# Fixing the engine order and putting all loads of an attention-plus-FFN kernel on one queue

The change has three parts. The program's own order of instructions is kept on every engine instead of a scheduler's. All loads go through one DMA queue in the order in which they are thought to be needed. The FFN weights arrive as f32 in column halves and are cast on GpSimd, where they had been cast to f16 by the DMA itself.

## Chip, cores and metric

One core of one Trainium2 chip. The metric is device time in microseconds (us), median of the runs. The kernel before takes 393.2 us (3 runs, 393.12 to 394.5).

## The reference

```python
def _attn_ref(q, k, v):                       # q, k, v: (8, 12, 448, 64) f32
    scores = (1 / sqrt(64)) * q @ k^T
    m = max(scores);  e = exp(scores - m)
    attn = e / (sum(e) + exp(-m) + 1e-9)      # = exp(s) / (sum exp(s) + 1)
    return attn @ v
# x = attention output as (3584, 768): token rows, 12 heads side by side
def _moe_ref(x, w1, w2, w3, w_out):           # each w 768 x 768 f32
    h = max(x @ w1, x @ w2, x @ w3)
    return h @ w_out
```

## The kernel before

A group is four heads of one batch; there are 24 groups, three per batch. Per group: load q, k, v (three tiles of 448 KB), cast to f16 on GpSimd, transpose q and k on TensorE, scores into PSUM, Exp on ScalarE (eight of 0.82 us), then denominator and numerator. Once three groups of a batch are done, the FFN pieces of that batch fill TensorE between the attention of the next. A first-layer piece is six matmuls, about 1.14 us.

```python
    def load_weight(i):                      # GpSimd's queue; the DMA casts f32 -> f16
        w = (moe_w1, moe_w2, moe_w3, moe_w_out)[i]
        if i < 3:
            src = w.rearrange("(hh gf dd) f -> hh dd gf f", hh=GH, dd=32)
            for hh in range(GH):             # four DMAs, 32 partitions each
                nc.gpsimd.dma_start(out=w_sb[i][hh*32 : hh*32+32], in_=src[hh])
        else:
            nc.gpsimd.dma_start(out=w_sb[i], in_=w.rearrange("(dc p) f -> p dc f", p=128))
# ... [cut: cast_group, transpose_group, scores_visit, av_group, up_piece, out_piece]
    cast_group(0)
    for i in range(4):
        load_weight(i)
    transpose_group(0)
    cast_group(1)
    for i in range(NI):                      # NI = 24 groups
        if i + 2 < NI: load_group(i + 2)     # SyncE's queue
        for vi, (pr, cs) in enumerate(visits):
            scores_visit(i, pr, cs)
            moe(per_visit)                   # FFN pieces that are due
            if vi == 0 and i > 0:
                av_group(i - 1)              # then add_pieces(b - 1) after each third group
            if vi == 2 and i + 1 < NI: transpose_group(i + 1)
        if i + 2 < NI: cast_group(i + 2)
```

The softmax here doesn't subtract the row's maximum and nothing guards it: scores larger than these inputs give would overflow.

Of the kernel before, what the change touches and what calls it, by code (L numbers as in the profile page):

```python
# [10 lines left out]
FP32 = mybir.dt.float32  # L11
FP16 = mybir.dt.float16
AF = mybir.ActivationFunctionType
ALU = mybir.AluOpType
ts = bass.ts

MMDT = FP16
LAMBDA = 256.0
# [3 lines left out]
def kernel(  # L22
# [11 lines left out]
    nc = tc.nc  # L34

    B, H, S, D = q.shape
    NTOK, DM = out.shape
    DFF = moe_w1.shape[1]
    SC = 112
    NCH = S // SC  # L40
    NDC = DM // 128
    NFC = DFF // 128
    GH = 4
    NG = H // GH
# [6 lines left out]
            name=nc.get_next_instruction_name(),  # L51
# [5 lines left out]

    cpool = ctx.enter_context(tc.tile_pool(name="const", bufs=1))
    ld_pool = ctx.enter_context(tc.tile_pool(name="ld", bufs=3))
    p16_pool = ctx.enter_context(tc.tile_pool(name="p16", bufs=2))  # L60
    v16_pool = ctx.enter_context(tc.tile_pool(name="v16", bufs=3))
    att_pool = ctx.enter_context(tc.tile_pool(name="att", bufs=4))
    e_pool = ctx.enter_context(tc.tile_pool(name="e", bufs=2))
    small = ctx.enter_context(tc.tile_pool(name="small", bufs=2))
    xt_pool = ctx.enter_context(tc.tile_pool(name="xt", bufs=2))
# [3 lines left out]
    ps1 = ctx.enter_context(tc.tile_pool(name="ps1", bufs=4, space=bass.MemoryType.PSUM))  # L69
    ps2 = ctx.enter_context(tc.tile_pool(name="ps2", bufs=2, space=bass.MemoryType.PSUM))  # L70

    groups = [(b, g) for b in range(B) for g in range(NG)]
    raw = {}

    def load_group(i):
        b, g = groups[i]
        tiles = []
        for name, src in (("q", q), ("k", k), ("v", v)):
            t = ld_pool.tile([SC, GH, NCH, D], FP32, tag="ld_" + name, name="ld_" + name)
            nc.sync.dma_start(  # L80
                out=t.rearrange("p h c d -> p h (c d)"),
                in_=src[b].rearrange(
                    "(h g) (p c) d -> g p h (c d)", g=NG, c=NCH
                )[g],
            )
            tiles.append(t)
        raw[i] = tiles

    load_group(0)
    load_group(1)  # L90

    ident16 = cpool.tile([128, 128], MMDT, name="ident16")
    make_identity(nc, ident16)
# [5 lines left out]
    w_sb = [cpool.tile([128, NDC, DFF], MMDT, name=f"w{i}") for i in range(4)]  # L99
    wout_sb = w_sb[3]  # L100

    def load_weight(i):
        w = (moe_w1, moe_w2, moe_w3, moe_w_out)[i]
        if i < 3:
            src = w.rearrange("(hh gf dd) f -> hh dd gf f", hh=GH, dd=32)
            for hh in range(GH):
                nc.gpsimd.dma_start(
                    out=w_sb[i][hh * 32 : hh * 32 + 32], in_=src[hh]
                )
        else:  # L110
            nc.gpsimd.dma_start(
                out=w_sb[i], in_=w.rearrange("(dc p) f -> p dc f", p=128)
            )


    state = {}

    def cast_group(i):
        qf, kf, vf = raw.pop(i)
        qk16 = []  # L120
        for pr in range(GH // 2):
            q16 = p16_pool.tile([SC, NCH, 2, D], MMDT, tag=f"q16_{pr}", name=f"q16_{pr}")
            k16 = p16_pool.tile([SC, NCH, 2, D], MMDT, tag=f"k16_{pr}", name=f"k16_{pr}")
            nc.gpsimd.tensor_copy(  # L124
                out=q16, in_=qf[:, 2 * pr : 2 * pr + 2].rearrange("p h c d -> p c h d")
            )
            nc.gpsimd.tensor_copy(  # L127
                out=k16, in_=kf[:, 2 * pr : 2 * pr + 2].rearrange("p h c d -> p c h d")
            )
            qk16.append((q16, k16))  # L130
        v16 = v16_pool.tile([SC, GH, NCH, D], MMDT, tag="v16", name="v16")
        nc.gpsimd.tensor_scalar(
            out=v16, in0=vf, scalar1=LAMBDA, scalar2=None, op0=ALU.mult
        )
        state[i] = {"qk16": qk16, "v16": v16}

    def transpose_group(i):
        st = state[i]
        st["qkT"] = []
        for pr in range(GH // 2):  # L140
            q16, k16 = st["qk16"][pr]
            trT = ps1.tile([128, 2, S], MMDT, tag="bank1", name="trT")
            for c in range(NCH):
                nc.tensor.transpose(  # L144
                    out=trT[:, 0, ts(c, SC)], in_=q16[:, c, :, :],
                    identity=ident16[0:SC, 0:SC],
                )
                nc.tensor.transpose(  # L148
                    out=trT[:, 1, ts(c, SC)], in_=k16[:, c, :, :],
                    identity=ident16[0:SC, 0:SC],  # L150
                )
            qkT = att_pool.tile([2 * D, 2, S], MMDT, tag="qkT", name="qkT")
            nc.vector.tensor_copy(out=qkT, in_=trT)  # L153
            st["qkT"].append(qkT)
        del st["qk16"]

    def scores_visit(i, pr, cs):
        st = state[i]
# [25 lines left out]
    def av_group(i):  # L184
        b, g = groups[i]
        st = state.pop(i)
        eT, v16 = st["eT"], st["v16"]
        if g == 0:
            xT[b] = xt_pool.tile([128, NDC, S], MMDT, tag="xT", name="xT")

        def col_tiled(weights):
            bank = ps1.tile([128, 512], FP32, tag="bank1", name="av")
            for c in range(NCH):
                for hh in range(GH):
                    nc.tensor.matmul(  # L195
                        out=bank[32 * hh : 32 * hh + 32, 0:S],
                        lhsT=weights(hh, c),
                        rhs=eT[:, hh, c, :],
                        start=(c == 0),
                        stop=(c == NCH - 1),  # L200
                    )
            return bank

        den = col_tiled(lambda hh, c: ones16[:, :])
        lnd = small.tile([128, S], FP32, tag="lnd", name="lnd")
        nc.scalar.activation(out=lnd, in_=den[:, 0:S], func=AF.Ln, bias=one_b)  # L206
        rb = small.tile([128, S], FP32, tag="rb", name="rb")
        nc.scalar.activation(out=rb, in_=lnd, func=AF.Exp, scale=-1.0)  # L208
        for hf in range(2):
            num = col_tiled(lambda hh, c: v16[:, hh, c, hf * 32 : hf * 32 + 32])  # L210
            nc.vector.tensor_tensor(  # L211
                out=xT[b][:, 2 * g + hf, :], in0=num[:, 0:S], in1=rb, op=ALU.mult
            )
# [23 lines left out]
    NH = 2  # L237
    NW = DM // NH
# [33 lines left out]
    pieces = []  # L272

    def add_pieces(b):
        for fc in range(NFC):
            for i in range(3):
                pieces.append((up_piece, (b, fc, i), NDC * S))
        for t in range(0, 3) if b % 2 == 0 else range(3, 7):
            for nh in range(NH):
                pieces.append((out_piece, (b // 2, t, nh), NFC * NW))  # L280

    credit = [0.0]

    def moe(cols):
        credit[0] += cols
        while pieces and credit[0] > 0:
            f, a, w = pieces.pop(0)
            f(*a)
            credit[0] -= w
        if not pieces:  # L290
            credit[0] = min(credit[0], 0.0)


    per_visit = (3 * NFC * NDC * S + 3.5 * NH * NFC * NW) / (NG * 4)
    cast_group(0)
    for i in range(4):
        load_weight(i)
    transpose_group(0)
    cast_group(1)

    visits = [(pr, cs) for pr in range(2) for cs in ((0, 1), (2, 3))]
    NI = len(groups)
    for i in range(NI):
        b, g = groups[i]
        if i + 2 < NI:
            load_group(i + 2)
        for vi, (pr, cs) in enumerate(visits):
            scores_visit(i, pr, cs)
            moe(per_visit)
            if vi == 0 and i > 0:  # L310
                av_group(i - 1)
                if g == 0:
                    add_pieces(b - 1)
            if vi == 2 and i + 1 < NI:
                transpose_group(i + 1)
        if i + 2 < NI:
            cast_group(i + 2)
    av_group(NI - 1)
    add_pieces(B - 1)
    moe(float("inf"))  # L320

# [29 lines left out]
```

## Time and profile before

| view | reading |
|---|---|
| busy time | TensorE (PE) 93% of a 390.9 us span |
| first FFN matmul | 51.0 us |
| after it | no gap in PE until 386.2 us; 14.75 us per group |
| longest wait of PE | 13.3 us, for the cast of group 1's q |

PE's waits, longest first: who waited, for what, us in total, times, longest.

```profile
...
PE trT L144 <- POOL q_0_162 L124: 13.3, 1, 13.3
PE trT L144 <- POOL q_0_117 L124: 5.9, 1, 5.9
...
```

GpSimd's own timeline says why that cast came so late: start us, length us, instruction, and in brackets the idle time before it and what ended it.

```profile
...
16.78 0.57 POOL L107 DMA_DIRECT2D w_115<-in_moe_w_dram  x1
21.48 0.57 POOL L107 DMA_DIRECT2D w_115<-in_moe_w_dram  x1 [4.13 <-DMA w_113<-in_moe_w_dram]
...
25.52 0.57 POOL L107 DMA_DIRECT2D w_115<-in_moe_w_dram  x1 [1.50 <-DMA w_113<-in_moe_w_dram]
27.61 0.85 POOL L111 DMA_DIRECT2D w_116<-in_moe_w_out_dram  x1 [1.52 <-DMA w_114<-in_moe_w_dram]
28.46 0.62 POOL L124 CAST q_0_162<-ld_q 112x512 f16<-112x512 f32 x1
...
```

GpSimd stands from 17 to 28 us with the issue of weight DMAs, each of which waits for an earlier one to land. The casts of group 1 (`q_0_162`) come behind them in its order. The data had come earlier: q, k and v of group 1 had landed by 15 us (issue at 2.2, 2.8 and 3.4 us, and 9.4, 10.5 and 11.5 us to landing).

The rates of the DMA engines in some stretches (the last column is GB/s, counted as bytes written): everything up to 49.5 us (the last weight landed at 51 us), weights and q, k, v together from 20 to 28 us, and q, k, v alone from 52 to 64 us.

```profile
...
core 0: us, PE busy (x) PEld busy (x) DVE busy (x) ACT busy (x) POOL busy (x), PEclk, DMA share, GB/s
2.00:49.50 47.50, 26.43 (x249) 11.91 (x253) 7.12 (x12) 23.01 (x31) 29.81 (x38) 1.00 1.13 247
20.00:28.00 8.00, 0.00 (x0) 0.00 (x0) 0.00 (x0) 0.00 (x0) 2.09 (x4) 1.00 1.14 241
52.00:64.00 12.00, 12.00 (x100) 5.91 (x102) 6.43 (x11) 6.19 (x9) 9.70 (x10) 1.00 1.13 274
...
```

Alone, q, k, v came at 274 GB/s.

### The profile page before, as it was taken

The page shows a single profiled execution, that of the slowest core. Times are in us where ns is not written, and L with a number is a line of the kernel's source. Part 1 is how long each engine was busy: PE and PEld are TensorE (multiplying, and loading weights), DVE is VectorE, ACT ScalarE, POOL GpSimd, SP SyncE. Part 2 cuts the span into 40 slices and gives each one's busy share as a digit, 9 for nine tenths or more (in the row PEclk, how much of TensorE's full clock was granted, in tenths as well). Part 3 has the DMA queues.
Part 4 walks back from the last instruction along what each step waited for, and adds up shares of the span by engine and source line. Part 5 has one row for each costly group of instructions (what it writes and reads, how often), then busy time and mean ns, then how long its engine had stood idle before and what let it go on. Part 6 is the DMA issues. An engine that isn't in the chain of part 4 may idle for free.

```text
span 390.9 us, 7477 instructions
## 1 busy us (share of the span) xinstructions
PE 363.1 (93%) x3120; PEld 180.1 (46%) x3120; DVE 174.8 (45%) x298; ACT 194.5 (50%) x241; POOL 129.7 (33%) x139
## 2 busy tenths in 40 slices
PE   2409999999999999999999999999999999999995
PEld 1104344554544554454554554454454554545552
DVE  0003244554454554454544544554554544544553
ACT  1606965556565555555565546556555546552000
POOL 3739666234252243243243233334243220000000
PEclk9999999999999999999999999999999999999998
DMA  8999999935614643527513663437100320004005
GB/s 196 272 240 236 239 285 268 250 85 187 143 47 96 198 152 96 134 71 201 143 47 96 162 189 96 117 74 216 49 3 0 82 82 0 2 0 123 2 0 162
DMA packets 41202, 49.24 MB, mean 126 GB/s; under 512 B 2256, under 2 KB 37584, under 8 KB 41168
## 3 DMA queue, kind: packets, MB, share of 16 engines
q1 hardware_dynamic: 37888, 44.05, 42.6%
q0 software_dynamic: 3280, 4.72, 6.6%
q8 instruction: 24, 0.39, 0.4%
q14 instruction: 10, 0.08, 0.1%
HBM read 42.47 MB, written 11.01 MB: 137 GB/s over the span
## 4 chain that ended last, share of the span: by engine, by line
PE 89%; ACT 2%; POOL 0%; DVE 0%; issue 0%
PE p_i L225 43%; PE op_ps L246 15%; PE av L195 15%; PE stp L166 12%; PE trT L148 2%; PE trT L144 2%; ACT eT L175 2%; ACT rb L208 0%; POOL k_0_163 L127 0%; DVE o_sb L253 0%; ACT lnd L206 0%
## 5 line engine op out<-in xcount | busy, mean ns | idle before, releaser
L175 ACT ACTIVATE eT<-stp 112x896 f16<-112x896 f32 x192 | 164.6, 916 | 126.7 <-PE stp L166 126.7
L235 DVE TENSOR_TENSOR hT<-hT,p_i 128x448 f16<-128x448 f16 x96 | 59.7, 621 | 68.4 <-PE p_i L225 68.3
L225 PE MATMUL p_i<-xT,w_114 128*128 128x448 f16 x288 | 62.9, 353 | 0.0
L225 PE MATMUL p_i<-xT,w_113 128*128 128x448 f16 x288 | 62.8, 353 | 0.0
L225 PE MATMUL p_i<-xT,w_115 128*128 128x448 f16 x288 | 62.5, 353 | 0.0
L166 PE MATMUL stp<-qkT 64*112 64x448 f16 x384 | 60.2, 383 | 1.9 <-ACT eT L175 1.9
L246 PE MATMUL op_ps<-w_116,hT 128*128 128x384 f16 x336 | 59.0, 327 | 0.0
L211 DVE TENSOR_TENSOR xT<-av,rb 128x448 f16<-128x448 f32 x48 | 27.7, 620 | 46.3 <-ACT rb L208 46.3
L253 DVE TENSOR_SCALAR o_sb<-op_ps 128x384 f32<-128x384 f32 x56 | 31.3, 558 | 34.2 <-PE op_ps L246 34.0
L233 DVE CAST hT<-p_i 128x448 f16<-128x448 f32 x48 | 30.0, 625 | 32.6 <-PE p_i L225 32.6
L246 PEld LDWEIGHTS <-hT 128*128 128x128 f16 x336 | 30.8, 98 | 27.0 <-issue 8.1
L153 DVE COPY qkT<-trT 128x896 f16<-128x896 f16 x48 | 27.8, 617 | 29.6 <-PE trT L148 29.6
L225 PEld LDWEIGHTS <-w_115 128*128 128x128 f16 x288 | 26.5, 98 | 29.6 <-issue 7.1
L225 PEld LDWEIGHTS <-w_114 128*128 128x128 f16 x288 | 26.5, 98 | 29.6 <-issue 7.1
L225 PEld LDWEIGHTS <-w_113 128*128 128x128 f16 x288 | 26.7, 98 | 28.9 <-issue 6.1
L166 PEld LDWEIGHTS <-qkT 64*112 64x112 f16 x384 | 18.6, 127 | 34.0 <-issue 24.7
L206 ACT ACTIVATE lnd<-av,one_b 128x448 f32<-128x448 f32 x24 | 15.3, 638 | 32.9 <-PE av L195 32.9
L195 PE MATMUL av<-eT,ones_109 112*32 112x448 f16 x384 | 25.8, 360 | 0.0
L195 PEld LDWEIGHTS <-ones_109 112*32 112x32 f16 x384 | 8.6, 96 | 14.1 <-issue 10.5
L208 ACT ACTIVATE rb<-lnd 128x448 f32<-128x448 f32 x24 | 13.9, 578 | 0.8
L144 PE MATMUL trT<-ident_104,q_0_162 112*128 112x112 f16 x4 | 0.9, 294 | 13.3 <-POOL q_0_162 L124 13.3
L144 PEld LDWEIGHTS <-q_0_162 112*128 112x128 f16 x4 | 0.5, 130 | 13.8 <-POOL q_0_162 L124 13.8
(371 smaller groups left out, 289.8 us busy)
## 6 DMA issues: line engine op xcount, KB each, us to landing
ld_q<-in_q_dram SPq DMA_DIRECT2D x24, 448.0 KB, 4.5
ld_k<-in_k_dram SPq DMA_DIRECT2D x24, 448.0 KB, 5.9
ld_v<-in_v_dram SPq DMA_DIRECT2D x24, 448.0 KB, 4.0
out_dram<-o_sb SPq DMA_DIRECT2D x8, 336.0 KB, 3.0
out_dram<-o_sb SPq DMA_DIRECT2D x8, 288.0 KB, 4.1
out_dram<-o_sb SPq DMA_DIRECT2D x8, 240.0 KB, 4.1
out_dram<-o_sb SPq DMA_DIRECT2D x8, 192.0 KB, 2.7
w_113<-in_moe_w_dram POOLq DMA_DIRECT2D x4, 288.0 KB, 9.1
```

Of the source, the lines that this page charges most:

```text
L153: nc.vector.tensor_copy(out=qkT, in_=trT)
L166: nc.tensor.matmul(out=stp[:, hh, 0:S], lhsT=qkT[hh * D : hh * D + D, 1, ts(c, SC)], rhs=qkT[hh * D : hh * D + D, 0, :], start=True, stop= ...
L175: nc.scalar.activation(out=st["eT"][:, 2 * pr : 2 * pr + 2, c, :], in_=stp[:, :, 0:S], func=AF.Exp, scale=scale,)
L195: nc.tensor.matmul(out=bank[32 * hh : 32 * hh + 32, 0:S], lhsT=weights(hh, c), rhs=eT[:, hh, c, :], start=(c == 0), stop=(c == NCH - 1),)
L206: nc.scalar.activation(out=lnd, in_=den[:, 0:S], func=AF.Ln, bias=one_b)
L208: nc.scalar.activation(out=rb, in_=lnd, func=AF.Exp, scale=-1.0)
L211: nc.vector.tensor_tensor(out=xT[b][:, 2 * g + hf, :], in0=num[:, 0:S], in1=rb, op=ALU.mult)
L225: nc.tensor.matmul(out=p_i[:, 0:S], lhsT=w_sb[i][:, dc, ts(fc, 128)], rhs=xT[b][:, dc, :], start=(dc == 0), stop=(dc == NDC - 1),)
L233: nc.vector.tensor_copy(out=dst, in_=p_i[:, 0:S])
L235: nc.vector.tensor_tensor(out=dst, in0=dst, in1=p_i[:, 0:S], op=ALU.max)
L246: nc.tensor.matmul(out=op_ps[:, 0:NW], lhsT=hT[bp][:, fc, ts(t, 128)], rhs=wout_sb[:, fc, ts(nh, NW)], start=(fc == 0), stop=(fc == NFC - 1),)
L253: nc.vector.tensor_scalar(out=o_sb[:, ts(nh, NW)], in0=op_ps[:, 0:NW], scalar1=1.0 / LAMBDA, scalar2=None, op0=ALU.mult,)
```

## The change

Its intent: no GpSimd time for issuing DMAs, no wait of casts behind weights, less waiting of TensorE by an order chosen by hand. The core of the diff, with cuts marked (pools, credits and the finer placing of FFN pieces are left out):

```diff
-    p16_pool ... bufs=2 ; v16_pool ... bufs=3
+    p16_pool ... bufs=4 ; v16_pool ... bufs=5
+    wst_pool = ctx.enter_context(tc.tile_pool(name="wst", bufs=2))
+    ctx.enter_context(tc.manual_schedule())
 ...
+    load_group(0, "qk", 2); load_group(1, "qk"); load_group(0, "v"); load_group(1, "v"); load_group(2)
 ...
-    def load_weight(i):
+    def load_weight(i, half):
+        cols = slice(half * FH, half * FH + FH)
+        wst = wst_pool.tile([128, NDC, FH], FP32, tag="wst", name="wst")
 ...
         if i < 3:
             for hh in range(GH):
-                nc.gpsimd.dma_start(out=w_sb[i][hh * 32 : hh * 32 + 32], in_=src[hh])
+                nc.sync.dma_start(out=wst[hh * 32 : hh * 32 + 32], in_=src[hh][:, :, cols])
+    def cast_weight(i, half):
+        nc.gpsimd.tensor_copy(out=w_sb[i][:, :, cols], in_=wst_of.pop((i, half)))
 ...
+        if i == 0:
+            cast_qk(2); cast_v(2)
+            for w in range(3):
+                load_weight(w, 0); cast_weight(w, 0)
+            load_group(3); cast_qk(3); cast_v(3)
+        elif i == 1:
+            for w in range(3):
+                load_weight(w, 1); cast_weight(w, 1)
+            load_group(4); cast_qk(4); cast_v(4)
+        elif i == 2:
+            for h in range(2):
+                load_weight(3, h); cast_weight(3, h)
+            load_group(5); cast_qk(5); cast_v(5)
 ...
-            if vi == 2 and i + 1 < NI:
-                transpose_group(i + 1)
+            elif vi < 3:                     # visits 1 and 2
+                moe((gap - tr_cols) / 2)
+                if i + 1 < NI:
+                    transpose_pair(i + 1, vi - 1)
+                moe((gap - tr_cols) / 2)
```

In TensorE's fixed order the transposes of group 3 stand in the middle of group 2's scores, and those of group 4 after the first two FFN pieces. On the queue, group 3 stands behind three weight halves and group 4 behind six.

More of the change, by code (lines that the diff above doesn't have):

```diff
@@ L59 @@
     ld_pool = ctx.enter_context(tc.tile_pool(name="ld", bufs=3))
-    p16_pool = ctx.enter_context(tc.tile_pool(name="p16", bufs=2))
-    v16_pool = ctx.enter_context(tc.tile_pool(name="v16", bufs=3))
+    p16_pool = ctx.enter_context(tc.tile_pool(name="p16", bufs=4))
+    v16_pool = ctx.enter_context(tc.tile_pool(name="v16", bufs=5))
     att_pool = ctx.enter_context(tc.tile_pool(name="att", bufs=4))
+    wst_pool = ctx.enter_context(tc.tile_pool(name="wst", bufs=2))
     e_pool = ctx.enter_context(tc.tile_pool(name="e", bufs=2))
@@ L70, with load_group @@
     ps2 = ctx.enter_context(tc.tile_pool(name="ps2", bufs=2, space=bass.MemoryType.PSUM))
+    ctx.enter_context(tc.manual_schedule())
     groups = [(b, g) for b in range(B) for g in range(NG)]
     raw = {}
-    def load_group(i):
+    def load_group(i, which="qkv", step=GH):
         b, g = groups[i]
-        tiles = []
-        for name, src in (("q", q), ("k", k), ("v", v)):
-            t = ld_pool.tile([SC, GH, NCH, D], FP32, tag="ld_" + name, name="ld_" + name)
-            nc.sync.dma_start(
-                out=t.rearrange("p h c d -> p h (c d)"),
-                in_=src[b].rearrange(
-                    "(h g) (p c) d -> g p h (c d)", g=NG, c=NCH
-                )[g],
-            )
-            tiles.append(t)
-        raw[i] = tiles
-    load_group(0)
-    load_group(1)
+        tiles = raw.setdefault(i, {})
+        for name in which:
+            tiles[name] = ld_pool.tile(
+                [SC, GH, NCH, D], FP32, tag="ld_" + name, name="ld_" + name
+            )
+        for h0 in range(0, GH, step):
+            for name in which:
+                src = {"q": q, "k": k, "v": v}[name][b].rearrange(
+                    "(h g) (p c) d -> g p h (c d)", g=NG, c=NCH
+                )[g]
+                nc.sync.dma_start(
+                    out=tiles[name][:, h0 : h0 + step].rearrange("p h c d -> p h (c d)"),
+                    in_=src[:, h0 : h0 + step],
+                )
+    load_group(0, "qk", 2)
+    load_group(1, "qk")
+    load_group(0, "v")
+    load_group(1, "v")
+    load_group(2)
     ident16 = cpool.tile([128, 128], MMDT, name="ident16")
@@ L100 @@
     wout_sb = w_sb[3]
-    def load_weight(i):
+    FH = DFF // 2
+    wst_of = {}
+    def load_weight(i, half):
         w = (moe_w1, moe_w2, moe_w3, moe_w_out)[i]
+        cols = slice(half * FH, half * FH + FH)
+        wst = wst_pool.tile([128, NDC, FH], FP32, tag="wst", name="wst")
+        wst_of[i, half] = wst
         if i < 3:
@@ L106, in load_weight, with cast_qk @@
             for hh in range(GH):
-                nc.gpsimd.dma_start(
-                    out=w_sb[i][hh * 32 : hh * 32 + 32], in_=src[hh]
-                )
-        else:
-            nc.gpsimd.dma_start(
-                out=w_sb[i], in_=w.rearrange("(dc p) f -> p dc f", p=128)
-            )
+                nc.sync.dma_start(
+                    out=wst[hh * 32 : hh * 32 + 32], in_=src[hh][:, :, cols]
+                )
+        else:
+            nc.sync.dma_start(
+                out=wst, in_=w.rearrange("(dc p) f -> p dc f", p=128)[:, :, cols]
+            )
+    def cast_weight(i, half):
+        cols = slice(half * FH, half * FH + FH)
+        nc.gpsimd.tensor_copy(out=w_sb[i][:, :, cols], in_=wst_of.pop((i, half)))
     state = {}
-    def cast_group(i):
-        qf, kf, vf = raw.pop(i)
+    def cast_qk(i):
+        qf, kf = raw[i].pop("q"), raw[i].pop("k")
         qk16 = []
@@ L130, in cast_group, with cast_v, transpose_pair @@
             qk16.append((q16, k16))
+        state[i] = {"qk16": qk16, "qkT": []}
+    def cast_v(i):
         v16 = v16_pool.tile([SC, GH, NCH, D], MMDT, tag="v16", name="v16")
         nc.gpsimd.tensor_scalar(
-            out=v16, in0=vf, scalar1=LAMBDA, scalar2=None, op0=ALU.mult
+            out=v16, in0=raw[i].pop("v"), scalar1=LAMBDA, scalar2=None, op0=ALU.mult
         )
-        state[i] = {"qk16": qk16, "v16": v16}
-    def transpose_group(i):
+        state[i]["v16"] = v16
+    def transpose_pair(i, pr):
         st = state[i]
-        st["qkT"] = []
-        for pr in range(GH // 2):
-            q16, k16 = st["qk16"][pr]
-            trT = ps1.tile([128, 2, S], MMDT, tag="bank1", name="trT")
-            for c in range(NCH):
-                nc.tensor.transpose(
-                    out=trT[:, 0, ts(c, SC)], in_=q16[:, c, :, :],
-                    identity=ident16[0:SC, 0:SC],
-                )
-                nc.tensor.transpose(
-                    out=trT[:, 1, ts(c, SC)], in_=k16[:, c, :, :],
-                    identity=ident16[0:SC, 0:SC],
-                )
-            qkT = att_pool.tile([2 * D, 2, S], MMDT, tag="qkT", name="qkT")
-            nc.vector.tensor_copy(out=qkT, in_=trT)
-            st["qkT"].append(qkT)
-        del st["qk16"]
+        q16, k16 = st["qk16"][pr]
+        trT = ps1.tile([128, 2, S], MMDT, tag="bank1", name="trT")
+        for c in range(NCH):
+            nc.tensor.transpose(
+                out=trT[:, 0, ts(c, SC)], in_=q16[:, c, :, :],
+                identity=ident16[0:SC, 0:SC],
+            )
+        for c in range(NCH):
+            nc.tensor.transpose(
+                out=trT[:, 1, ts(c, SC)], in_=k16[:, c, :, :],
+                identity=ident16[0:SC, 0:SC],
+            )
+        qkT = att_pool.tile([2 * D, 2, S], MMDT, tag="qkT", name="qkT")
+        nc.vector.tensor_copy(out=qkT, in_=trT)
+        st["qkT"].append(qkT)
     def scores_visit(i, pr, cs):
@@ L276, in add_pieces @@
             for i in range(3):
-                pieces.append((up_piece, (b, fc, i), NDC * S))
+                pieces.append((up_piece, (b, fc, i), NDC * (S + 6)))
         for t in range(0, 3) if b % 2 == 0 else range(3, 7):
             for nh in range(NH):
-                pieces.append((out_piece, (b // 2, t, nh), NFC * NW))
+                pieces.append((out_piece, (b // 2, t, nh), NFC * (NW + 6)))
     credit = [0.0]
@@ L291, in moe @@
             credit[0] = min(credit[0], 0.0)
-    per_visit = (3 * NFC * NDC * S + 3.5 * NH * NFC * NW) / (NG * 4)
-    cast_group(0)
-    for i in range(4):
-        load_weight(i)
-    transpose_group(0)
-    cast_group(1)
+    UP = NDC * (S + 6)
+    OUT = NFC * (NW + 6)
+    per_group = (3 * NFC * UP + 3.5 * NH * OUT) / NG
+    av_cols = 3 * NCH * (S + 6) + 480
+    tr_cols = 2 * NCH * SC
+    gap = (per_group + av_cols + 2 * tr_cols) / 4
     visits = [(pr, cs) for pr in range(2) for cs in ((0, 1), (2, 3))]
@@ L302 @@
     NI = len(groups)
+    cast_qk(0)
+    cast_qk(1)
+    cast_v(0)
+    cast_v(1)
+    transpose_pair(0, 0)
+    transpose_pair(0, 1)
     for i in range(NI):
         b, g = groups[i]
-        if i + 2 < NI:
-            load_group(i + 2)
+        if i == 0:
+            cast_qk(2)
+            cast_v(2)
+            for w in range(3):
+                load_weight(w, 0)
+                cast_weight(w, 0)
+            load_group(3)
+            cast_qk(3)
+            cast_v(3)
+        elif i == 1:
+            for w in range(3):
+                load_weight(w, 1)
+                cast_weight(w, 1)
+            load_group(4)
+            cast_qk(4)
+            cast_v(4)
+        elif i == 2:
+            for h in range(2):
+                load_weight(3, h)
+                cast_weight(3, h)
+            load_group(5)
+            cast_qk(5)
+            cast_v(5)
+        elif i + 3 < NI:
+            load_group(i + 3)
+            cast_qk(i + 3)
+            cast_v(i + 3)
@@ L307 @@
         for vi, (pr, cs) in enumerate(visits):
             scores_visit(i, pr, cs)
-            moe(per_visit)
-            if vi == 0 and i > 0:
-                av_group(i - 1)
-                if g == 0:
-                    add_pieces(b - 1)
-            if vi == 2 and i + 1 < NI:
-                transpose_group(i + 1)
-        if i + 2 < NI:
-            cast_group(i + 2)
+            if vi == 0:
+                spare = gap - av_cols
+                moe(spare / 2)
+                if i > 0:
+                    av_group(i - 1)
+                moe(spare / 2)
+                if i > 0 and g == 0:
+                    add_pieces(b - 1)
+            elif vi < 3:
[3 more added lines that the diff above has]
+                moe((gap - tr_cols) / 2)
+            else:
+                moe(gap)
```

## The prediction

> **What bounds the kernel now.** TensorE. The page's busy table gives PE 93% of a 390.9 us span, and the chain of waits is 89% PE. From the first FFN matmul (51.0 us) to the last (386.2 us) PE has no gap: one group of four heads costs 14.75 us, 91.4 to 135.6 us being three of them. After that only a 4.7 us write-out. The change cannot win there: matmuls, tiling switches and tail are the same ones. Only the head, 0 to 51 us, can move.
>
> **Head before.** The wait view: PE waits 5.9 us for the first q cast, then 13.3 us (15.8 to 29.1) for the q cast of group 1. That data had landed (queue 1 moved about 4 MB by 18 us); GpSimd was stuck issuing weight DMAs, each waiting for an earlier one, so its casts came late. Then ScalarE paces two groups (7.8 us each: eight Exp of 0.82, Ln, Exp).
>
> **What the change does.** It removes the weight issues from GpSimd (the 13.3 us hole) and adds eight weight casts there, about 2.5 us each (estimate from 512 columns in 0.61 us), off the critical path. It doubles what the weights write: 4.7 MB of f16 becomes 9.4 MB of f32. And PE's order is now fixed: transposes of group 3 come before scores of group 2 are finished, those of group 4 right after the first two FFN pieces. But on the single queue group 3 stands behind three weight halves and group 4 behind six.
>
> **Arrival sum.** q/k/v alone ran at 275 GB/s (52 to 64 us), 1.67 us a tile. 14 tiles must land before group 4 can be transposed: 23.4 us, plus 3.5 us of start and landing, plus six weight halves of 1.18 MB. Each w1..w3 DMA writes 32 partitions. [...]
>
> **On the critical path.** First transposes about 1.5 us earlier; hole gone; group 1 and 2 run on ScalarE's pace to about 27 us. Then PE waits for group 3's k cast until about 39 us, FFN starts near 48 us (before: 51.0, with exactly the same work done), and after two pieces PE waits again until about 60.5 us for group 4. Before, the equal state was reached at 53.3 us. Net: loss of 7 us[...]. A fixed order also costs about 1 us at batch ends (division waits behind Exps). Group 5 and w_out come in time.
>
> **Prediction:** 400 us, 8 in 10 between 388 and 405. Faster by over 2%: 0.08; within 2%: 0.47; slower by over 2%: 0.45.
>
> **What would show it.** PE's waits: no 13.3 us wait for group 1; instead two for GpSimd casts of groups 3 (about 12 us) and 4 (about 10 us). The 40 slices: queue full from 2 to 65 us[...]. First FFN matmul near 48 us, a hole after its second piece. From about 65 us a group again costs 14.75 us.
>
> **What would make it wrong.** Weight halves arriving faster (above 390 GB/s would make it over 2% faster) or slower; weight casts much over 2.5 us, which would hold back the reuse of the two staging buffers; new PE stalls in the steady part because a fixed order cannot fill waits.

In the arrival sum the rate assumed for the weight halves and its alternative are cut, and so is what rested on them further on: no trace of this case that the prediction had shows them. The sum came to near 60 us for group 4's k: 23.4 us of tiles, 3.5 us of start and landing, and a remainder of about 33 us for the six halves. The 390 GB/s near the end of the text is an estimate from the same sum: six halves at that rate take about 18 us instead of 33.

## More of the kernel before

From the page of the kernel before. In the rows of slices each digit is the busy tenth of 1/40 of the span; PEclk is the granted TensorE clock in tenths; the last row is what the DMA engines wrote, in GB/s.

```profile
span 390.9 us, 7477 instructions
...
PE 363.1 (93%) x3120; PEld 180.1 (46%) x3120; DVE 174.8 (45%) x298; ACT 194.5 (50%) x241; POOL 129.7 (33%) x139
...
PE   2409999999999999999999999999999999999995
...
PEclk9999999999999999999999999999999999999998
...
GB/s 196 272 240 236 239 285 268 250 85 187 143 47 96 198 152 96 134 71 201 143 47 96 162 189 96 117 74 216 49 3 0 82 82 0 2 0 123 2 0 162
...
```

Apart from the write-out at the end, only the head is not full: the first three slices (29 us).

## The result

| | before | after |
|---|---|---|
| median, us | 393.2 | 407.93 (407.56 to 410.06) |
| ratio | | 1.0379, interval 1.0315 to 1.0443: slower |
| first FFN matmul, us | 51.0 | 53.6 |
| first k cast of group 3 / group 4, us | 39.0 / 46.9 | 42.6 / 65.6 |
| written by the DMA engines, mean | 247 GB/s (2 to 49.5 us) | 235 GB/s (2 to 78 us) |

A ratio is the mean time of one kernel's fast runs over the mean of the other's fast runs of the same rounds, so it is not quite the ratio of the medians quoted.

The page of the changed kernel, same lines:

```profile
span 405.8 us, 7489 instructions
...
PE 369.1 (91%) x3120; PEld 180.6 (45%) x3120; DVE 173.9 (43%) x298; ACT 193.1 (48%) x241; POOL 139.1 (34%) x134
...
PE   3980755999999999999999999999999999999995
...
PEclk9996585999999999999999999999999999999999
...
GB/s 195 221 210 216 219 212 303 272 265 47 180 260 88 2 101 265 200 2 40 232 231 26 0 205 274 89 1 88 237 204 2 36 121 2 2 0 118 2 0 156
...
```

The hole of before is gone from slices 2 and 3. In its place stand two, from 31 to 42 us (slices 4 and 5) and from 56 to 64 us (slices 6 and 7), and the granted clock falls in them and is a half just after each (0.50 from 41.5 to 53 us and from 64.4 to 69 us). From slice 8 on both kernels look alike. PE's waits:

```profile
...
PE trT L165 <- POOL q_0_206 L144: 10.9, 1, 10.9
PE trT L165 <- POOL q_0_295 L144: 8.4, 1, 8.4
PE trT L165 <- POOL q_0_130 L144: 4.5, 1, 4.5
...
PE trT L170 <- POOL k_0_296 L147: 1.3, 1, 1.3
PE trT L170 <- POOL k_0_207 L147: 1.2, 1, 1.2
...
```

`q_0_206` is group 3, `q_0_295` is group 4. GpSimd's timeline around them: the casts of weights (`w_126` to `w_128` are w1 to w3) wait for their DMAs, and the two groups come after the weights in arrival and in order.

```profile
...
28.57 2.10 POOL L133 CAST w_126<-wst 128x2304 f16<-128x2304 f32 x1 [3.87 <-DMA wst<-in_moe_w_dram]
33.52 2.11 POOL L133 CAST w_127<-wst 128x2304 f16<-128x2304 f32 x1 [2.85 <-DMA wst<-in_moe_w_dram]
38.85 2.11 POOL L133 CAST w_128<-wst 128x2304 f16<-128x2304 f32 x1 [3.22 <-DMA wst<-in_moe_w_dram]
40.90 0.61 POOL L144 CAST q_0_206<-ld_q 112x512 f16<-112x512 f32 x1
42.62 0.61 POOL L147 CAST k_0_207<-ld_k 112x512 f16<-112x512 f32 x1 [1.10 <-DMA ld_k<-in_k_dram]
...
50.30 2.10 POOL L133 CAST w_126<-wst 128x2304 f16<-128x2304 f32 x1 [2.96 <-DMA wst<-in_moe_w_dram]
55.92 2.11 POOL L133 CAST w_127<-wst 128x2304 f16<-128x2304 f32 x1 [3.52 <-DMA wst<-in_moe_w_dram]
61.71 2.11 POOL L133 CAST w_128<-wst 128x2304 f16<-128x2304 f32 x1 [3.69 <-DMA wst<-in_moe_w_dram]
63.82 0.61 POOL L144 CAST q_0_295<-ld_q 112x512 f16<-112x512 f32 x1
65.63 0.61 POOL L147 CAST k_0_296<-ld_k 112x512 f16<-112x512 f32 x1 [1.20 <-DMA ld_k<-in_k_dram]
...
```

The rates: q, k, v alone (10 to 20 us), weight halves into 32 partitions at a time (22 to 30 and 46 to 60 us), w_out into 128 partitions (67.5 to 71.5 us).

```profile
...
2.00:78.00 76.00, 46.19 (x356) 20.62 (x360) 14.78 (x24) 31.30 (x40) 42.92 (x34) 0.80 1.10 235
10.00:20.00 10.00, 9.07 (x64) 3.80 (x65) 1.25 (x2) 8.35 (x11) 8.28 (x7) 1.00 1.15 220
22.00:30.00 8.00, 6.06 (x80) 2.93 (x78) 1.74 (x3) 7.56 (x10) 4.13 (x2) 1.00 1.11 216
46.00:60.00 14.00, 9.48 (x72) 3.54 (x69) 2.79 (x5) 6.45 (x9) 5.55 (x3) 0.74 1.11 207
67.50:71.50 4.00, 4.00 (x23) 1.61 (x22) 0.81 (x3) 1.73 (x2) 3.76 (x2) 0.68 1.06 372
...
```

The halves come at 216 and 207 GB/s, w_out at 372, and q, k, v alone at 220, not at the 274 that the kernel before showed.

Where the 14.7 us come from (14.9 us between the two profiled spans). Before any experiment the two traces can be lined up. When the changed kernel starts the FFN, exactly the same matmuls have been done as in the kernel before at its FFN start. The first two pieces end at 53.3 us before; after, group 4's k can be transposed at 66.3 us: 13.0 us lost. From there to the end it takes 405.8 - 66.3 = 339.5 us, against 390.9 - 53.3 = 337.6 us before: 1.9 us more, and all of it lies in the first 5 us, in which the clock is still halved (0.50 to 69 us; the run with the longer fill, below, shows this). The steady part costs the same.

### The profile page after: what moved, and what is told of

It is laid out like the page before. It is cut to its first block, busy times and chain, and to the rows that moved or that the text cites. A ratio compares the mean times of both kernels' runs of the same rounds, so it can differ in the third digit from the quotient of the medians.

```text
span 405.8 us, 7489 instructions
## 1 busy us (share of the span) xinstructions
PE 369.1 (91%) x3120; PEld 180.6 (45%) x3120; DVE 173.9 (43%) x298; ACT 193.1 (48%) x241; POOL 139.1 (34%) x134
## 4 chain that ended last, share of the span: by engine, by line
PE 82%; DMA 10%; SPq 4%; POOL 1%; issue 0%; DVE 0%; POOLq 0%
PE p_i L246 42%; PE op_ps L267 14%; PE av L216 12%; PE stp L187 11%; DMA wst<-in_moe_w_dram 8%; SPq L90 3%; DMA ld_k<-in_k_dram 2%; PE trT L170 2%; PE trT L165 2%; SPq L123 2%; POOL w_126 L133 1%; POOL k_0_296 L147 0%; DVE o_sb L274 0%; POOLq L133 0%; POOLq L147 0%
## 5 line engine op out<-in xcount | busy, mean ns | idle before, releaser
L187 PE MATMUL stp<-qkT 64*112 64x448 f16 x384 | 62.0, 393 | 3.9 <-ACT eT L196 3.9
L246 PE MATMUL p_i<-xT,w_126 128*128 128x448 f16 x288 | 63.2, 353 | 0.0
L175 DVE COPY qkT<-trT 128x896 f16<-128x896 f16 x48 | 29.6, 617 | 37.4 <-PE trT L170 37.4
L246 PEld LDWEIGHTS <-w_128 128*128 128x128 f16 x288 | 26.2, 99 | 28.8 <-issue 8.5
L246 PEld LDWEIGHTS <-w_127 128*128 128x128 f16 x288 | 25.9, 98 | 28.3 <-issue 8.0
L246 PEld LDWEIGHTS <-w_126 128*128 128x128 f16 x288 | 26.1, 98 | 27.8 <-issue 6.9
L216 PE MATMUL av<-eT,ones_122 112*32 112x448 f16 x384 | 24.1, 373 | 0.0
L165 PE MATMUL trT<-ident_117,q_0_206 112*128 112x112 f16 x4 | 0.6, 294 | 10.9 <-POOL q_0_206 L144 10.9
L144 POOL CAST q_0_3529<-ld_q 112x512 f16<-112x512 f32 x1 | 0.6, 611 | 27.3 <-DMA ld_q<-in_q_dram 27.3
```

Of the source, the lines that this page charges most:

```text
L175: nc.vector.tensor_copy(out=qkT, in_=trT)
L187: nc.tensor.matmul(out=stp[:, hh, 0:S], lhsT=qkT[hh * D : hh * D + D, 1, ts(c, SC)], rhs=qkT[hh * D : hh * D + D, 0, :], start=True, stop= ...
L216: nc.tensor.matmul(out=bank[32 * hh : 32 * hh + 32, 0:S], lhsT=weights(hh, c), rhs=eT[:, hh, c, :], start=(c == 0), stop=(c == NCH - 1),)
L246: nc.tensor.matmul(out=p_i[:, 0:S], lhsT=w_sb[i][:, dc, ts(fc, 128)], rhs=xT[b][:, dc, :], start=(dc == 0), stop=(dc == NDC - 1),)
```

## The experiments

The theories. **A**: the queue delivers groups 3 and 4 too late, because of how many bytes it must write first and how fast; the fixed order only makes TensorE wait for them. **B**: the fixed order itself costs the time. **C**: the f32 bytes or the GpSimd casts cost it, in whatever order they come. **D**: the halved clock after the waits (0.50 until 53 us and until 69 us) costs it. **E**: the two staging buffers starve the queue. **F** (about the kernel before): its head is bound by bytes, not by GpSimd's issues. All medians are of three rounds unless said.

### Without the fixed order

```diff
-    ctx.enter_context(tc.manual_schedule())
```

> The changed kernel without the line that fixes the order: the scheduler that ordered the kernel before orders each engine again; loads and casts stay as changed. Theory A (late arrival of groups 3 and 4, which stand behind the weights on one queue): casts of group 3 near 41 us and of group 4 near 64 us as in the changed kernel, PE still waits for both, time 404 to 408 us. Rival B (the fixed order of TensorE costs the time): back to 390 to 394 us.

Measured: 405.73 us, ratio 1.0325 (1.0289 to 1.0361). Group 3's k is cast at 42.95 us, group 4's at 64.96. The scheduler moved the rest of group 2's scores ahead of group 3's transposes, and the FFN starts at 49.9 us instead of 53.6, but then waits for group 4 all the same. B falls as the main cause: about 2 of the 14.7 us went with the order, hardly clear of noise (the intervals of the two ratios overlap), and 0.7 us of them is an earlier arrival of group 4.

### Groups 3 and 4 ahead of the weights

```diff
-            for w in range(3): load_weight(w, 0); cast_weight(w, 0)
             load_group(3); cast_qk(3); cast_v(3)
+            for w in range(3): load_weight(w, 0); cast_weight(w, 0)
 ... (the same for group 4 and the second halves)
```

> Same bytes, queue, casts and TensorE order; only groups 3 and 4 are loaded (and cast) ahead of the three weight halves that preceded them. Theory A: no wait for group 3, group 4 cast about 17 us earlier (near 48 us), now the third weight half (near 46 us) and the last halves (near 67 us) are what PE waits for, at about 2 us each; time 389 to 394 us. Rival C (the amount of f32 bytes or the GpSimd casts, whatever their order): still above 400 us.

Measured: 407.48 us, ratio 1.0356 (1.0341 to 1.0372). A miss. The first half came as expected: no wait for group 3, FFN at 40.7 us, group 4's k at 48.6 (after a wait of 4.9 us for its q). The waits for weights that were expected did not come. Instead TensorE stood 13.5 us for group 5, whose k is cast at 80.2 us (78.0 in the changed kernel):

```profile
...
79.22 0.56 PE L165 MATMUL trT<-ident,q 112*128 112x112 f16 x4 [13.53 <-POOL q L144]
...
```

That corrected theory A. The order only chooses which group is late. Through group 5 the queue must write six groups (8.26 MB) and all weights as f32 (9.44 MB), 17.7 MB; at the 235 GB/s of the changed kernel this takes 75 us. The kernel before writes its weights as 4.72 MB. C, as worded ("still above 400"), is right here.

### The same bytes into 128 partitions

Wrong result on purpose: rows of the weights go to the wrong partitions.

```diff
-            src = w.rearrange("(hh gf dd) f -> hh dd gf f", hh=GH, dd=32)
-            for hh in range(GH):
-                nc.sync.dma_start(out=wst[hh * 32 : hh * 32 + 32], in_=src[hh][:, :, cols])
+            src = w.rearrange("(dc p) f -> p dc f", p=128)
+            for d0 in range(0, NDC, 2):
+                nc.sync.dma_start(out=wst[:, d0 : d0 + 2], in_=src[:, d0 : d0 + 2, cols])
```

> Wrong result on purpose: the halves of w1, w2, w3 are read in plain row order, so that each of three DMAs writes all 128 partitions (393 KB each) instead of four DMAs that write 32 partitions each (295 KB each); bytes, row pieces of 1536 B, order and casts are unchanged. Theory A[...]: a half takes 3.2 to 3.6 us instead of 5.65, the weight stretches run at 330 to 370 GB/s as w_out did in the changed kernel, group 4 can be transposed near 52 us, time 392 to 397 us. If 1536 B pieces are slow for another reason: rate stays near 209 GB/s and time near 408 us.

Measured: 401.38 us, ratio 1.0204 (1.0174 to 1.0233). Windows of its trace: two stretches of weights, and the one between them that the expectation had not foreseen.

```profile
...
22.00:26.00 4.00, 2.73 (x28) 1.49 (x25) 1.63 (x3) 3.93 (x5) 2.29 (x2) 1.00 1.05 364
26.00:30.00 4.00, 3.32 (x54) 1.62 (x55) 0.20 (x1) 3.74 (x6) 3.11 (x2) 1.00 0.26 80
42.00:46.00 4.00, 3.43 (x22) 1.55 (x24) 0.62 (x1) 3.94 (x5) 3.44 (x2) 0.50 1.06 373
...
```

The rate is as expected, 364 and 373 GB/s where the changed kernel had 216 and 207, with the same 1536-byte pieces and the same bytes. So in this case the rate goes with the partitions that each DMA writes. The DMAs also grew by a third, from 295 to 393 KB, but the loads of q, k, v, which are larger still (459 KB), ran at 214 to 274 GB/s, so size alone does not make the difference. The time is not as expected: from 26 to 30 us the queue is nearly idle (80 GB/s), because the third half waits for a staging buffer, that is for the cast of the first (25.95 to 28.05 us).

### Unused matmuls in the waits

`fill(n)` (its definition is left out) issues n unused matmuls of 448 columns.

```diff
+                    if vi == 1 and i in (2, 3):
+                        fill({2: 48, 3: 40}[i])      # second run: {2: 54, 3: 70}
                     transpose_pair(i + 1, vi - 1)
```

> 48 unused matmuls before the transposes of group 3 and 40 before those of group 4 keep TensorE busy in its two waits. Theory D (the granted clock of 0.5 after the waits costs time of its own): granted clock 1.0 throughout, FFN starts about 3 us earlier (near 50 us) but then only waits longer for group 4, and the stretch after group 4's transposes shrinks by about 2 us: 405.3 to 406.5 us. Were the half clock the main cause: below 398 us.

Measured: 406.91 us, ratio 1.0368 (1.0324 to 1.0412), 0.4 us above the expected range. The clock still fell (0.50 from 46 to 50 us and from 66 to 68 us), so this run decides little. With a longer fill:

> The changed kernel with more unused matmuls (54 and 70) before the transposes of groups 3 and 4; with 48 and 40 the granted clock had still fallen to 0.5 from 45 to 52 and 65 to 69 us. Theory D: clock 1.0 after 60 us, the six matmuls after group 4's transposes take 1.2 us instead of 2.4, time 404.5 to 406.5 us, so the half clock is worth 1.5 to 3 us of the 14.7 lost.

Measured: 404.83 us, ratio 1.0316 (1.0266 to 1.0366). The same six matmuls after group 4's transposes, in the timeline of PE (start, length, instruction; x6 is a count), first in the changed kernel:

```profile
...
66.30 0.56 PE L170 MATMUL trT<-ident_117,k_0_296 112*128 112x112 f16 x4 [1.25 <-POOL k_0_296 L147]
66.64 2.45 PE L246 MATMUL p_i<-xT,w_128 128*128 128x448 f16 x6
...
```

And in the run with the longer fill:

```profile
...
64.92 0.36 PE L170 MATMUL trT<-ident,k 112*128 112x112 f16 x4
65.12 1.30 PE L246 MATMUL p_i<-xT,w 128*128 128x448 f16 x6
...
```

They take 2.45 us in the changed kernel, at a granted clock of 0.50, and 1.30 us with the longer fill, where the clock row of the page shows 0.9 or more in that slice. Between group 4's k transposes and its second pair of transposes lie 4.99 us in the changed kernel (66.30 to 71.29) and 3.09 us here (64.92 to 68.01), and from there 402.7 - 64.92 = 337.8 us remain, as before the change. So the half clock costs 1.9 us. The rest of the 3 us that this run gained is an earlier arrival of group 4 (63.2 us), not the clock. D is a small part.

### Three staging buffers

```diff
-    wst_pool = ctx.enter_context(tc.tile_pool(name="wst", bufs=2))
+    wst_pool = ctx.enter_context(tc.tile_pool(name="wst", bufs=3))
```

> The changed kernel with three staging buffers for the f32 weights instead of two. In its trace the queue fell to 145 GB/s for 2 us (30 to 32 us) because the third half waited for the cast of the first. Theory A (the queue's rate into 32 partitions): that gives back at most 1 us, 406 to 408 us. Rival E (the reuse of the staging buffers is what starves the queue): below 402 us.

Measured: 409.94 us, ratio 1.0425 (1.0406 to 1.0443); no gain, 2 us above the expected range. The dip at 30 to 32 us is gone (215 GB/s from 28 to 34 us), but q, k, v ran at only 214 GB/s in this profile and group 4's k came at 66.8 us. E is refuted as the main cause. Why the time is not a little better stays open. With 128 partitions it is another matter:

> Wrong result on purpose, as with the 128-partition loads before, now with three staging buffers. With halves of 3.2 us the queue had stood at about 80 GB/s from 26 to 30 us and below 185 from 46 to 50 us, waiting for casts. Theory A with staging as the second limit: those gaps close, group 4's transposes come 3 to 6 us earlier (near 54 us instead of 58 to 59), time 394 to 398 us. If staging does not matter: 401 us as before.

Measured: 395.98 us (wrong result again), ratio 1.0075 (1.0046 to 1.0104), group 4's k at 53.2 us. As expected: with halves of 3.2 us (1.18 MB at 364 to 373 GB/s), two buffers were too few: 401.38 us with two, 395.98 with three.

### The kernel before with one DMA for each weight

Heads of a group are made neighbours and d is split into even and odd, so that partition p of a weight chunk is row 2p plus a constant, and one DMA can fill 128 partitions. The result is correct.

```diff
-  "(h g) (p c) d -> g p h (c d)"
+  "(g h) (p c) d -> g p h (c d)"
-            for hh in range(GH):
-                nc.gpsimd.dma_start(out=w_sb[i][hh * 32 : hh * 32 + 32], in_=src[hh])
+            nc.gpsimd.dma_start(out=w_sb[i].rearrange("p (g hf) f -> p g hf f", hf=2),
+                                in_=w.rearrange("(g p hf) f -> p g hf f", g=NG, hf=2))
 ... (v is cast into a tile with even and odd d apart, and the numerator reads it so)
```

> The kernel before, correct result, with only the layout of heads and of the split of d changed, so that each weight is one casting DMA into 128 partitions (4 DMAs on GpSimd instead of 13). Theory A: GpSimd no longer waits for DMAs in flight, so the 13.3 us wait of TensorE for group 1 is gone; written bytes stay 4.7 MB for the weights; the FFN starts at 38 to 43 us instead of 51; time 381 to 387 us. Rival F (the head is bound by bytes alone, not by GpSimd's queue of issues): FFN starts near 50 us, time 391 to 394 us.

Measured: 397.38 us, ratio 1.01 (1.0061 to 1.0139). A miss. The wait for group 1 is down from 13.3 to 4.4 us, and two others take its place, 6.2 and 4.6 us, both for group 3. The FFN starts at 57.8 us in the profiled run (399.55 us, the slowest of the four); with the granted clock at 0.50 from 44 to 52 us, it takes 13.9 us from group 3's k cast to the FFN, 12.0 in the kernel before. PE's waits in this run:

```profile
...
PE trT L143 <- POOL q L123: 15.8, 3, 6.2
PE trT L147 <- POOL k L126: 6.6, 5, 4.6
...
```

The four weight DMAs now share the DMA engines with q, k, v without a break (227 to 242 GB/s in every 2 us from 16 to 44 us). Group 3's k is cast at 44.0 us, group 2's at 24.95: three tiles (1.38 MB) in 19.0 us are 72 GB/s, while the engines wrote about 233 GB/s in all. How the engines divide their time between the two queues no run here shows. It seems, though no run isolates it, that GpSimd's blocked issues, which looked like the whole trouble of the kernel before, had also kept the weights from crowding out q, k, v (group 3's k was cast at 39.0 us there). F is nearer the truth than A was.

### The changed kernel with casting DMAs

Fixed order and the order of q, k, v as in the changed kernel; no staging and no GpSimd casts of weights; four casting DMAs in the layout above, w1 to w3 issued after the casts of group 1, w_out later.

> The changed kernel with fixed order and with its order of q, k, v, but the weights go by four casting DMAs from GpSimd straight to f16, no staging, no GpSimd casts (same layout change as in the run above, correct result). Theory A (f32 staging doubles the bytes written to 14 MB of 17.7 MB through group 5, at about 235 GB/s): group 3 is cast by 33 to 38 us, group 4 by 47 us, time 385 to 392 us. Rival B (fixed order): above 400 us.

(A slip in that text: the weights' f32 bytes are 9.4 of the 17.7 MB; 14 MB is wrong.) Measured: 390.08 us, ratio 0.9925 (0.989 to 0.996), correct. Group 3's k at 27.3 us, FFN at 40.8, group 4's k at 46.0 with a wait of 3.2 us. With the fixed order kept, the time is below the kernel before, so B falls a second time as the main cause. What of this gain is due to half the bytes, to 128 partitions or to the second queue that the weights now have (GpSimd's), this run does not separate. The GpSimd casts of weights, the other half of C, were not the limit in the changed kernel: its timeline above shows GpSimd idle for 2.9 to 3.9 us before each of the six, waiting for the DMA.

### One weight at a time

```diff
-    for w in range(3): load_weight(w)         # after cast_v(1)
+    load_weight(0)                            # after cast_v(1)
             cast_qk(3); cast_v(3)
+            load_weight(1)
             cast_qk(4)
+            load_weight(2)
-        for fc in range(NFC):
-            for i in range(3):
+        for i in range(3):
+            for fc in range(NFC):
                 pieces.append((up_piece, (b, fc, i), ...))
```

> As the run with casting DMAs and the fixed order, but w1, w2, w3 are issued one after another between the casts of groups 1 and 4, and the first-layer pieces run weight by weight instead of column by column, so each weight is needed later. Theory A (bytes in front of what TensorE needs next): group 4's k is cast by 38 to 43 us instead of 46, the 3.2 us wait for it goes, granted clock stays 1.0 after 45 us; time 383 to 388 us, correct. If the wait only moves to w2 or w3: 389 to 391 us.

Five rounds. Measured: 383.17 us (382.18 to 384.63), ratio 0.9737 (0.9707 to 0.9768), correct: faster than both kernels. PE's waits:

```profile
...
PE trT L152 <- POOL q L131: 5.5, 2, 4.1
...
```

And the head of its page:

```profile
span 380.8 us, 7453 instructions
...
PE   3877999999999999999999999999999999999994
...
PEclk9988999999999999999999999999999999999999
...
```

The first 4.1 us are the very start. Group 4's k is cast at 35.2 us, the FFN starts at 40.4 us, 10.5 us earlier than before, and the time is 10.3 us shorter. Which of the two edits matters more, the later issue of weights or the new order of pieces, no run separates.

### The kernel before, profiled again

> The kernel before, profiled a second time. In its first trace q, k, v alone ran at 274 GB/s (52 to 64 us) and 270 (10 to 20 us), from which the prediction took 275; the same first eleven loads in the same order ran at 214 to 238 GB/s in the profiles of the changed kernel and of the runs derived from it. If 270 to 275 comes back, the rate belongs to this kernel's loads; if it shows 215 to 250, it differs from execution to execution and 275 was one draw. The 13.3 us wait for group 1 and 393 us should come back either way.

Measured, one look: 394.44 us. PE's waits were of the same kind (14.5 us for group 1), and q, k, v ran slower. The rates from 10 to 20 us (some weights are under way there too) and from 52 to 64 us (q, k, v alone):

```profile
...
10.00:20.00 10.00, 4.45 (x16) 1.22 (x12) 0.46 (x1) 6.60 (x8) 7.24 (x9) 1.00 1.14 253
52.00:64.00 12.00, 12.00 (x82) 5.87 (x79) 6.42 (x11) 7.72 (x10) 10.06 (x10) 1.00 1.13 252
...
```

253 and 252 GB/s where the first profile had 270 and 274. In the changed kernel and the runs derived from it the stretch from 10 to 20 us showed 214 to 260 GB/s, with the same loads in the same order in most of them. This profile is from another chip (4) than most of the runs, but six runs on chip 1 with the same first loads (the first six variants of the changed kernel) differ among themselves too, 214 to 235 GB/s. So this rate differs from one execution to the next; what sets it was not found.

## Why the prediction was wrong

The direction was right (a loss of 7 us, to 400 us, was predicted). The size was not: 407.9 us lies above the range of 388 to 405. The step that failed is the arrival time of group 4: its tiles of q, k, v were taken to come faster than they did, and the halved clock after its wait was left out.

- **Hole removed, two new waits: right.** Predicted about 12 us for group 3 and about 10 us for group 4. The wait table shows 10.9 + 1.2 us and 8.4 + 1.3 us. That these lengths fit so well is partly luck: the first wait began and ended almost 4 us later than predicted (30.7 instead of 27 us, 42.6 instead of 39), the second almost 6 us later (56.1 to 66.3 instead of about 50.3 to 60.5), so the errors at the two ends cancel.
- **The time of the six weight halves: right.** Their casts follow each other, or the v tile before them, by 6.6, 5.0, 5.3, 5.7, 5.6 and 5.8 us, 34.1 us in all where the forecast's sum left 33. The rate behind those 33 us was an assumption that nothing in the trace of before could show. This case shows 207 and 216 GB/s in such stretches, and 364 to 373 with 128 partitions. The 128-partition run tied the rate to the partitions; what lies behind that no run here shows.
- **"q/k/v alone ran at 275 GB/s ..., 1.67 us a tile": this is the term that was mis-sized.** Group 4's k cast began at 65.6 us. Less 34.1 us of halves and 3.5 us of start, 28.0 us remain for 14 tiles, 2.0 us a tile or 229 GB/s, 4.6 us more than predicted. The loss is spread evenly: 2.0 us a tile for the nine up to group 2's v (cast at 21.9 us), 1.9 for group 3's three, 2.0 for group 4's two. One stretch of one execution had been taken as a constant; a second profile of the same kernel showed 252.
- **The halved clock was left out.** After each long wait the matmuls ran slower (four transposes in 0.56 us instead of 0.36 after both waits, six matmuls in 2.45 us instead of 1.30 after the second): 1.9 us on the critical path, measured as the difference between the changed kernel and the one with the longer fill. The granted clock fell to 0.50 within these waits of 10.9 and 8.4 us. The prediction did not count it. The clock row of before gave no hint, with 0.9 or more up to the last slice, although the transposes after the long wait of before followed each other at about half the later rate too (by 0.09 us, later by 0.05).
- **About 1 us at batch ends by the fixed order: not seen.** After group 4's transposes 337.8 us remain in the run with the longer fill, in which the clock was not halved at that point (0.9 or more), against 337.6 before.

The sum of the miss: group 4's transposes came at 66.3 us instead of 60.5, which is 5.8 us (tiles 4.6, halves 1.1), and the clock took 1.9 us, together 7.7 of the 7.9 us by which 407.9 exceeds 400.

What the change cost as a whole, by the runs: f32 through staging and into 32 partitions. From 407.9 us, writing to 128 partitions gives 401.4, a third staging buffer then 396.0, f16 from the DMA without staging 390.1, and spreading the weights 383.2. These steps are not independent (the third buffer alone gave nothing), and the last two also changed the layout of heads and moved the weights to a second queue. The order fixed by the program cost about 2 us at most by the medians (the run without it); whether it helps once the data come in time no run shows, since the fastest kernel was not run without it.

## What to carry to other kernels

When loads bound the head of a kernel, count the bytes written through the point where each group is needed, and take the rate for the partitions that each DMA writes (here 207 to 216 GB/s into 32, 364 to 373 into 128). Reordering the one full queue here only moved the wait to another tile (13.5 us for group 5). The casting DMAs wrote half the bytes of the f32 staging copy (4.72 MB instead of 9.44), and not all weights needed to be there when the first piece started: order the pieces so that each weight is needed later, and issue it later (390.1 us to 383.2 by both edits here). Take a rate from several executions before a sum rests on it (274 and 252 GB/s here for the same loads).

## Further measurements of this case

- 1024-byte pieces into 112 partitions (q, k, v alone, one queue) ran at 214 to 274 GB/s, and 1536-byte pieces into 128 partitions at 364 to 373; no run separates piece size from partitions. The same loads of one program ran at 274 and 252 GB/s in two executions.
- In the kernel before the clock record says 1.0 from 2 to 49.5 us, while after its 13.3 us wait the transposes follow each other by 0.09 us (29.77, 29.86, 29.95 us) and later by 0.05 us (36.04, 36.09, 36.14 us). So here the record alone does not show what the spacing shows.
- GpSimd took 0.61 us for a cast of 112 x 512 from f32 to f16, 2.1 us for 128 x 2304, and 2.77 us for 112 x 1024 with a multiplication (v).
- Beside the casting DMAs on the other queue, 72 of about 233 GB/s were left to the plain loads of q, k, v (the kernel before with one DMA for each weight, 25 to 44 us).
